# Decode attention with a gated dense layer: GpSimd brings the output projection's chunks with two or four partitions per DMA engine, in whole 32 KB elements

## The chip, the core and the metric

The kernel runs on one core of a Trainium2 chip. The core has TensorE (matrix products), VectorE, ScalarE, GpSimd and SyncE, each with its own instruction queue, and 16 DMA engines that all queues share. The metric is the device time of one execution in microseconds: 192.6 us before, the median of three runs (192.58 to 192.64).

## What is computed

One token is decoded. Branch A is attention of one query against a cache of 4096 positions for 32 heads of 128, followed by the output projection `wo`; branch B is a dense layer with a squared ReLU; a gate mixes the two.

```python
def reference(A_x, A_k_cache, A_v_cache, A_wq, A_wo, B_x, B_w1, B_b1, B_w2, B_b2, gate_w):
    # x [1,1,512], k_cache and v_cache [1,32,4096,128], wq [512,4096], wo [4096,512]
    q = (x @ wq) as [1,32,1,128]
    scores = einsum("bhqd,bhkd->bhqk", q, k_cache) * 128 ** -0.5
    o = einsum("bhqk,bhkd->bhqd", softmax(scores), v_cache)
    a = o as [1,1,4096] @ wo
    h = relu(x @ w1 + b1) ** 2          # w1 [512,1376]
    b = h @ w2 + b2                     # w2 [1376,512]
    g = sigmoid((x * gate_w).sum())
    return g * a + (1 - g) * b          # everything in bfloat16
```

The two caches are 32 MB each; with the weights nearly 79 MB are read, each byte once.

## The kernel before

The heads go in eight tiles of four. For each tile the kernel loads 4 MB of K and 4 MB of V into a ring of five slots (`ring`), 128 partitions of 32 KB each. SyncE issues these loads in the order of `LOADS`, each after the slot's old contents are no longer read (`free`): for a K tile the counts of VectorE and TensorE, for a V tile those of TensorE. Loads are issued well ahead, and the transfers queue.

The scores of a tile are split by position. VectorE does 80 of 128 blocks (96 in the last tile) with a multiply and add along the row (`ttr`, L704); TensorE transposes the rest (L502), ScalarE copies the transposes out of PSUM (L408) and TensorE multiplies them with the query (L515). Then come the maximum (L711, L522, L718, L721, L527), the exponentials on ScalarE (L427) and the products with V on TensorE (`pv`, L546), some two tiles later.

The projection `wo` comes in two parts. Heads 0 to 27 (3.5 MB) are seen as 112 chunks of 32 rows, 32 KB each, and every chunk goes to one partition of `W`, a tile that first holds `wq`. Which chunk lies on which partition is free, since a selection matrix `selA` puts the attention output on the same partitions: `spread_a` multiplies with it (L565), and then TensorE (`out_a`, L573) and VectorE (`rows_v`, L766 and L770) use `W`. The last four heads of `wo` go elsewhere, at the very end, on SyncE's queue (L332), with the last 128 rows of `w2` behind them (L334).

The plan of the chunks is by DMA engine. `INNER` names partitions 32 to 95, engine e having 32 + 4e to 35 + 4e; `OUTER` the partitions 0 to 31 and 96 to 127, also four per engine; `SEAM` is a pair of them (31 and 99). An entry of `RUNS` is a kind, the first engine e, the number of engines k, which of the four partitions r, and in the kernel before a factor m: with m = 2 the run brings two partitions per engine. `place` turns it into first partition, step and count. Engines 0 to 2 are filled by `FIRST`, eight transfers of three chunks each that SyncE issues (L320). Engine 3 gets one chunk, engines 0 to 2, 4, 7 and 8 eight each, and the others seven.

The runs are GpSimd's. A transfer of GpSimd begins at the engine where the one before ended, so `turns` puts in a dummy (L368, a few bytes into `dm`) wherever the next run is to begin elsewhere, with as many engines as are to be skipped. GpSimd first builds `selA` with one `affine_select` per strip (L356), waits until `W` is free and the gate and bias are done (`started`, L310), then issues dummies and runs in order (L368, L371), waits for all of them (L377, L378) and sets `tick` (L379), whose semaphore `s_wk` lets `spread_a` and `rows_v` go on. `max_dma_last_dim=16384` on the runs cuts each 32 KB row into two elements of 16 KB.

SyncE's order around this: wq (L290), three K tiles and the first V tile (L326), the eight transfers of `FIRST` (L320), then the other K and V tiles; V of the last three tiles comes in parts (L324); before the last V come `w1` and `w2` (L329, L330).

Of the kernel before, what the change touches and what calls it, by code (L numbers as in the profile page):

```python
# [5 lines left out]
def bass_gated_mix__gqa_block_cached__dense_activation_squared_relu__decode_kernel(  # L6
# [50 lines left out]
    for i in (28, 29, 30):  # L57
# [20 lines left out]
    TP = 32 - TV  # L78
    TM = 6
    INNER, OUTER, SEAM = range(3)  # L80
    RUNS = [(INNER, 4, 12, 0, 2), (INNER, 4, 12, 1, 2),
            (OUTER, 4, 4, 0, 1), (OUTER, 8, 8, 0, 1), (OUTER, 4, 4, 1, 1), (OUTER, 8, 8, 1, 1),
            (OUTER, 4, 4, 2, 1), (OUTER, 8, 8, 2, 1),
            (OUTER, 3, 2, 3, 1), (SEAM, 7, 2, 3, 1)]
    FIRST = [(INNER, 0, 3, 0, 1), (INNER, 0, 3, 1, 1), (INNER, 0, 3, 2, 1), (INNER, 0, 3, 3, 1),
             (OUTER, 0, 3, 0, 1), (OUTER, 0, 3, 1, 1), (OUTER, 0, 3, 2, 1), (OUTER, 0, 3, 3, 1)]

    def place(kind, e, k, r, m):
        if kind == INNER:
            return 32 + 4 * e + r, 4 // m, k * m  # L90
        if kind == OUTER:
            return (4 * e if e < 8 else 64 + 4 * e) + r, 4, k
        return 28 + r, 68, k

    def turns():
        at, out = 0, []
        for _, e, k, _, _ in RUNS:
            d = (e - at) % 16
            out.append((False, d) if d != 1 else (True, e))
            at = (e + k) % 16  # L100
        return out

    def strips():
        q = 0
        for run in RUNS + FIRST:
            yield (*place(*run), q)
            q += place(*run)[2]
        assert q == 4 * NA

    STRIPS = list(strips())  # L110

    k_v = A_k_cache.rearrange("a (j r) (p b) d -> (a j) (r p) (b d)", r=R, p=P)
    v_v = A_v_cache.rearrange("a (j r) (p b) d -> (a j) (r p) (b d)", r=R, p=P)
    wq_v = A_wq.rearrange("(p t) n -> p (t n)", t=4)
    woa_v = A_wo.rearrange("(p t) n -> p (t n)", t=32)
# [15 lines left out]
    with ctx:  # L131
        def sb(name, shape, dt):
            return ctx.enter_context(nc.sbuf_tensor(name, shape, dt))
# [4 lines left out]
        def sem(name):  # L138
            return ctx.enter_context(nc.semaphore(name))
# [3 lines left out]
        def held(kind, j=0):  # L143
            return ring[:, AT[kind, j] % SLOTS, :]

        W = sb("W", [128, 32 * DM], bf16)
# [32 lines left out]
        o2f = sb("o2f", [128, TV], fp32)  # L179
        dm = sb("dm", [16, len(RUNS), 2, 6], bf16)  # L180
        ident = sb("ident", [128, 128], bf16)
# [54 lines left out]
        s_wo = [sem(f"s_wo{n}") for n in range(len(TS) - 1)]  # L236
        s_wp = [sem(f"s_wp{n}") for n in range(len(RUNS))]
        s_dm = [sem(f"s_dm{n}") for n in range(len(RUNS))]
        s_wr = sem("s_wr")
# [56 lines left out]
        def free(eng, n):  # L296
            if n < SLOTS:
                return
            kind, j = LOADS[n - SLOTS]
            if kind == "k":  # L300
                eng.wait_ge(s_sd, U * (j + 1))
                eng.wait_ge(s_t, 2 * U * (j + 1))
            elif kind == "v":
                eng.wait_ge(s_pv, U * (j + 1))

        def started(eng):
            eng.wait_ge(s_qps, NT)
            eng.wait_ge(s_g, 4)
            eng.wait_ge(s_b1c, 1)  # L310

        @block.sync
        def _(eng):
            for n, (kind, j) in enumerate(LOADS):
                free(eng, n)
                if n == SLOTS - 1:
                    started(eng)
                    for p, st, k, q in STRIPS[len(RUNS):]:
                        eng.dma_start(W[p:p + st * (k - 1) + 1:st, :], woa_v[q:q + k, :]).then_inc(s_wr, 16)  # L320
                if kind == "v" and j in PARTS:
                    for w in range(len(PARTS[j]) - 1):
                        part = slice(PARTS[j][w] * 128, PARTS[j][w + 1] * 128)
                        eng.dma_start(held("v", j)[:, part], v_v[j][:, part]).then_inc(s_vl[j, w], 16)  # L324
                elif kind in "kv":
                    eng.dma_start(held(kind, j), (k_v if kind == "k" else v_v)[j])\  # L326
                       .then_inc(s_l[n % SLOTS], 16)
                elif kind == "m":
                    eng.dma_start(held("m")[:, 0:W2], w1_v).then_inc(s_w[0], 16)  # L329
                    eng.dma_start(held("m")[:, W2:W3], w2_v).then_inc(s_w[1], 16)  # L330
            for c in range(len(TS) - 1):
                eng.dma_start(wob_sb[:, TS[c]:TS[c + 1], :], wob_v[:, TS[c]:TS[c + 1], :])\  # L332
                   .then_inc(s_wo[c], 16)
            eng.dma_start(w2b, B_w2[F - 128:F, :]).then_inc(s_w[2], 16)  # L334
            eng.wait_ge(s_f4, 1)
            eng.dma_start(out[0, 0, :].rearrange("(j p) -> j p", p=128), fin4).then_inc(s_out, 16)

        @block.gpsimd
        def _(eng):  # L340
            eng.memset(ident[:, :], 0.0).then_inc(s_id, 1)
            eng.memset(identf[:, :], 0.0).then_inc(s_id, 1)
            eng.memset(onesf[:, :], 1.0).then_inc(s_cst, 1)
            eng.wait_ge(s_id, 2)
            for m in (ident, identf):
                eng.affine_select(out=m[:, :], in_=m[:, :], compare_op=ALU.not_equal, fill=1.0,
                                  base=0, pattern=[[-1, 128]], channel_multiplier=1)\
                   .then_inc(s_id, 1)
            eng.memset(RS[:, :], 0.0).then_inc(s_cst, 1)
            eng.memset(E[:, :, :, :], 0.0).then_inc(s_cst, 1)  # L350
            eng.memset(selA[:, :, :], 0.0).then_inc(s_sel, 1)
            eng.wait_ge(s_sel, 1)
            for n, (p, st, k, q) in enumerate(STRIPS):
                eng.wait_ge(s_sel, n + 1)
                part = selA[:, :, p:p + st * (k - 1) + 1]
                eng.affine_select(out=part, in_=part, compare_op=ALU.not_equal, fill=1.0, base=-st * q,  # L356
                                  pattern=[[st, 4], [-1, st * (k - 1) + 1]], channel_multiplier=4 * st)\
                   .then_inc(s_sel, 1)

            started(eng)
            sent = 0
            for n, ((back, d), run) in enumerate(zip(turns(), RUNS)):
                if back:
                    eng.inc_swdge_sem([], [], mode="reset_dge_cursor")
                if d:
                    src = B_w1[0:d, 0:32].rearrange("p (a c) -> p a c", a=2)
                    eng.dma_start(dm[0:d, sent, :, 0:4], src[:, :, 0:4]).then_inc(s_dm[sent], 16)  # L368
                    sent += 1
                p, st, k, q = STRIPS[n]  # L370
                eng.dma_start(W[p:p + st * (k - 1) + 1:st, :], woa_v[q:q + k, :],  # L371
                              max_dma_last_dim=16384).then_inc(s_wp[n], 16)
            for n in range(sent):
                eng.wait_ge(s_dm[n], 16)
            eng.wait_ge(s_wr, 16 * len(FIRST))
            for q in s_wp[:-1]:
                eng.wait_ge(q, 16)  # L377
            eng.wait_ge(s_wp[-1], 16)  # L378
            eng.memset(tick[:, :], 0.0).then_inc(s_wk, 1)  # L379
# [461 lines left out]
```

## Time and profile before

| | |
|---|---|
| median of three runs | 192.60 us |
| the profiled execution: its time, its span | 192.64 us, 191.2 us |
| VectorE busy | 158.8 us (83%) |
| TensorE busy | 111.2 us (58%) |
| ScalarE busy | 82.6 us (43%) |
| GpSimd busy | 18.7 us (10%) |
| DMA, mean over the span | 412 GB/s, 78.74 MB in 5300 packets |
| granted TensorE clock | 0.58 |
| GpSimd's DMAs | 17: 10 runs and 7 dummies, issued from 33.8 to 43.8 us |
| `FIRST`, issued by SyncE | 33.5 to 39.2 us |

A line of the waits names who waited, for whom, and how long in all, how often and the longest. A line of the timeline or of the chain starts with the start and the duration in us. The page's queue rows give packets, MB and the share of the time of 16 engines; the trace also keeps each packet's queue, start, duration and size.

### The profile page before, as it was taken

The numbers are of one execution on the slowest core, as the hardware profiler recorded it, in microseconds if no ns is written. First come the engines' busy times: TensorE is split into PE (matmuls) and PEld (weight loads), VectorE is DVE, ScalarE is ACT, GpSimd is POOL, SyncE is SP. The second block draws the span as 40 slices with busy tenths as digits, with TensorE's granted clock in tenths as the row PEclk, the third lists the DMA queues.
The fourth block names the chain that finished last, engine by engine and source line by source line (L and its number), as shares of the span: only waits on it lengthen the run. The fifth ranks groups of instructions, "written<-read, shape, count | busy, mean of one in ns | idle before, by whom it ended". The sixth has DMA issues, their size and how long they took to land.

```text
span 191.2 us, 5991 instructions
## 1 busy us (share of the span) xinstructions
PE 111.2 (58%) x2058; PEld 97.6 (51%) x2058; DVE 158.8 (83%) x1387; ACT 82.6 (43%) x204; POOL 18.7 (10%) x48
## 2 busy tenths in 40 slices
PE   0139567645614653397469254936876478548975
PEld 0123244535503542297359244935866368537964
DVE  0310399999999999999999998999999699998821
ACT  2105675843833663078339232943743393000400
POOL 7630000991000000000000000000000000000000
PEclk9999995855555555555555555555555555555555
DMA  6999999999999999999999999999999999999992
GB/s 220 440 439 439 439 441 429 439 401 454 422 413 418 432 420 418 449 413 446 422 437 422 432 417 411 441 417 439 435 427 429 391 425 413 422 417 425 418 383 82
DMA packets 5300, 78.74 MB, mean 412 GB/s; under 512 B 1099, under 2 KB 1741, under 8 KB 1870
## 3 DMA queue, kind: packets, MB, share of 16 engines
q1 hardware_dynamic: 4488, 75.47, 93.1%
q0 software_dynamic: 768, 2.89, 3.7%
q8 instruction: 16, 0.26, 0.6%
q14 instruction: 14, 0.11, 0.1%
q10 hardware_dynamic: 14, 0.01, 0.0%
HBM read 78.35 MB, written 0.00 MB: 410 GB/s over the span
## 4 chain that ended last, share of the span: by engine, by line
DVE 64%; DMA 25%; SPq 7%; issue 1%; PE 1%; DVEq 0%
DVE ring L704 60%; DMA ring<-in_A_wo_dram 14%; DMA ring<-in_A_k_cache_dram 11%; SPq L324 7%; DVE S L704 3%; DVE gm L718 1%; PE pM L555 1%; DVE gx L721 0%; PE pQ L607 0%; DVE mp L711 0%; SPq L330 0%; DVE rden L728 0%; SPq L290 0%; SPq L329 0%; DVE qcol L693 0%
## 5 line engine op out<-in xcount | busy, mean ns | idle before, releaser
L704 DVE CUSTOM_DVE_ANT_0 ring<-ring,qb 128x128 bf16<-128x128 bf16 x656 | 140.6, 283 | 1.8 <-DMA ring<-in_A_k_cache_dram 1.8
L408 ACT ACTIVATE kT<-KP 128x768 bf16<-128x768 bf16 (+1 forms) x64 | 46.4, 783 | 47.2 <-PE KP L502 46.9
L502 PE MATMUL KP<-ident,ring 128*128 128x128 bf16 x368 | 43.5, 302 | 18.9 <-DMA ring<-in_A_k_cache_dram 15.7
L704 DVE DVE_READ_ACCUMULATOR2_ANT S<- 128x1 f32 x656 | 52.0, 79 | 0.1
L502 PEld LDWEIGHTS KP<-ident,ring 128*128 128x128 bf16 x368 | 36.0, 140 | 21.5 <-DMA ring<-in_A_k_cache_dram 16.1
L546 PE MATMUL pO<-E,ring 128*128 128x4 bf16 x640 | 19.5, 166 | 3.8 <-DMA ring<-in_A_v_cache_dram 2.1
L546 PEld LDWEIGHTS pO<-E,ring 128*128 128x128 bf16 x640 | 18.7, 105 | 4.3 <-DMA ring<-in_A_v_cache_dram 2.4
L427 ACT ACTIVATE E<-S,nM 32x128 bf16<-32x128 f32 x32 | 18.5, 579 | 1.0
L546 PE MATMUL pX<-E,ring 128*128 128x4 bf16 x384 | 12.0, 167 | 4.7 <-DMA ring<-in_A_v_cache_dram 4.7
L546 PEld LDWEIGHTS pX<-E,ring 128*128 128x128 bf16 x384 | 11.4, 105 | 5.2 <-DMA ring<-in_A_v_cache_dram 5.1
L522 PE MATMUL pM<-identf,mp 128*1 128x128 f32 x8 | 3.0, 379 | 14.5 <-DVE mp L711 14.5
L419 ACT ACTIVATE nM<-pM 128x1 f32<-128x1 f32 x8 | 1.4, 171 | 23.0 <-PE pM L527 23.0
L527 PE MATMUL pM<-onesf,gx 1*128 1x1 f32 x16 | 4.7, 358 | 9.0 <-DVE gx L721 9.0
L527 PEld LDWEIGHTS pM<-onesf,gx 1*128 1x128 f32 x16 | 4.0, 307 | 9.6 <-DVE gx L721 9.6
L522 PEld LDWEIGHTS pM<-identf,mp 128*1 128x1 f32 x8 | 0.7, 85 | 16.0 <-DVE mp L711 15.8
L515 PE MATMUL pQ<-qcol,kT 128*128 128x4 bf16 x176 | 7.8, 170 | 1.0 <-ACT kT L408 0.9
L515 PEld LDWEIGHTS pQ<-qcol,kT 128*128 128x128 bf16 x176 | 7.6, 111 | 1.3 <-ACT kT L408 1.3
L515 PE MATMUL pS<-qcol,kT 128*128 128x4 bf16 x192 | 8.1, 169 | 0.0
L427 ACT ACTIVATION_READ_ACCUMULATOR E<-S,nM 32x1 f32 x32 | 8.1, 253 | 0.0
L515 PEld LDWEIGHTS pS<-qcol,kT 128*128 128x128 bf16 x192 | 7.9, 108 | 0.2
L399 ACT ACTIVATE qb<-pQ 32x128 bf16<-32x128 f32 x16 | 4.3, 268 | 7.8 <-PE pQ L480 7.5
L555 PE MATMUL pM<-RS,onesf 128*128 128x8 f32 (+1 forms) x10 | 2.9, 358 | 7.8 <-DVE gm L718 6.6
(83 smaller groups left out, 94.2 us busy)
## 6 DMA issues: line engine op xcount, KB each, us to landing
ring<-in_A_k_cache_dram SPq DMA_DIRECT2D x8, 4096.0 KB, 29.9
ring<-in_A_v_cache_dram SPq DMA_DIRECT2D x5, 4096.0 KB, 29.0
W<-in_A_wq_dram SPq DMA_DIRECT2D x1, 4096.0 KB, 12.2
ring<-in_A_v_cache_dram SPq DMA_DIRECT2D x2, 2048.0 KB, 27.5
ring<-in_A_v_cache_dram SPq DMA_DIRECT2D x4, 1024.0 KB, 28.2
ring<-in_A_v_cache_dram SPq DMA_DIRECT2D x2, 1280.0 KB, 32.3
W<-in_A_wo_dram POOLq DMA_DIRECT2D x2, 768.0 KB, 18.1
ring<-in_B_w_dram SPq DMA_DIRECT2D x1, 1376.0 KB, 25.7
```

Source lines behind the costliest of these rows:

```text
L324: eng.dma_start(held("v", j)[:, part], v_v[j][:, part]).then_inc(s_vl[j, w], 16)
L399: eng.activation(qb[rows, c, :], QR[c % 2][rows, r * 128:r * 128 + 128], ACT.Copy)\
L408: eng.activation(kT[:, n % NC, 0:HB[u // U] * 128], KP[n % 3][:, 0:HB[u // U] * 128], ACT.Copy).then_inc(s_ev, 1)
L427: eng.activation(E[rows, j % NE, :, r], S[rows, j % NS, :], ACT.Exp, bias=nM[rows, j:j + 1], scale=SCALE, accum_out=RS[rows, R * j + r:R * ...
L502: mm = eng.transpose(KP[n % 3][:, y * 128:(y + 1) * 128], held("k", j)[:, b * 128:(b + 1) * 128], ident[:, :])
L515: mm = eng.matmul(S2[j % 2][:, c:c + R], kT[:, n % NC, y * 128:(y + 1) * 128], qcol[:, R * j:R * j + R], start=True, stop=True)
L522: eng.transpose(MT[0:1, :], mp[:, j:j + 1], identf[:, :]).then_inc(s_mt, 1)
L527: eng.matmul(MB[:, j:j + 1], gx[0:1, j % 2, :], onesf[0:1, 0:1], start=True, stop=True).then_inc(s_mb, 1)
L546: mm = eng.matmul(O(R * j, R * j + R), held("v", j)[:, b * 128:(b + 1) * 128], E[:, j % NE, b, :], start=(b == 0), stop=(b == B - 1), skip ...
L555: eng.matmul(DEN[:, a:b], onesf[:, :], RS[:, a:b], start=True, stop=True).then_inc(s_den, 1)
L704: ins = eng.tensor_tensor_reduce(kb, kb, qb[:, j, :], 1.0, 0.0, ALU.mult, ALU.add, S[:, j % NS, b:b + 1])
L718: eng.tensor_reduce(g, MT[0:1, :].rearrange("a (r p) -> a r p", r=R), AX.X, ALU.max)\
```

## The change

`RUNS` names the partitions of an engine as a tuple: the first run brings all four `INNER` partitions of engines 4 to 15 (48 chunks in one transfer), the next two bring partitions 0 and 2 of the `OUTER` group, and four runs of one partition per engine remain. Seven runs are left, and `turns` then gives five dummies. For a run of several partitions the source rows are rearranged so that its outermost dimension counts the engines and the next one the partitions of each; the destination is one strip of partitions. The rows are no longer cut: `max_dma_last_dim` is gone, and an element is 32 KB. Which partition belongs to which engine, and how many chunks each engine gets, is as before; which chunk lies on which partition changes, and `selA` is built from `ROWS`, which has a strip for each partition index r of a run: 12 strips for the runs and 8 for `FIRST`, where there were 10 and 8.

```diff
-    RUNS = [(INNER, 4, 12, 0, 2), (INNER, 4, 12, 1, 2),
-            (OUTER, 4, 4, 0, 1), (OUTER, 8, 8, 0, 1), (OUTER, 4, 4, 1, 1), (OUTER, 8, 8, 1, 1),
-            (OUTER, 4, 4, 2, 1), (OUTER, 8, 8, 2, 1),
-            (OUTER, 3, 2, 3, 1), (SEAM, 7, 2, 3, 1)]
+    RUNS = [(INNER, 4, 12, (0, 1, 2, 3)), (OUTER, 4, 4, (0, 2)), (OUTER, 8, 8, (0, 2)),
+            (OUTER, 4, 4, (1,)), (OUTER, 8, 8, (1,)), (OUTER, 3, 2, (3,)), (SEAM, 7, 2, (3,))]
...
+    def place(kind, e, k, rs):
+        r, m = rs[0], len(rs)
+        if kind == SEAM:
+            return 28 + r, 68, k, m
+        p = 32 + 4 * e + r if kind == INNER else (4 * e if e < 8 else 64 + 4 * e) + r
+        return p, 4 // m, k, m
...
     STRIPS = list(strips())
+    ROWS = [(p + st * r, st * m, k, q + r * k) for p, st, k, m, q in STRIPS for r in range(m)]
...
-            for n, (p, st, k, q) in enumerate(STRIPS):
+            for n, (p, st, k, q) in enumerate(ROWS):
                 eng.wait_ge(s_sel, n + 1)
...
-                p, st, k, q = STRIPS[n]
-                eng.dma_start(W[p:p + st * (k - 1) + 1:st, :], woa_v[q:q + k, :],
-                              max_dma_last_dim=16384).then_inc(s_wp[n], 16)
+                p, st, k, m, q = STRIPS[n]
+                rows = woa_v[q:q + k * m, :]
+                if m > 1:
+                    rows = rows.rearrange("(r i) n -> i r n", r=m)
+                eng.dma_start(W[p:p + st * (k * m - 1) + 1:st, :], rows).then_inc(s_wp[n], 16)
```

## The prediction

> **What bounds the kernel now.** I read the DMA row of the slices and the queue rows first, then the chain of waits, the table of waits, GpSimd's timeline, the busy time by stage, and last the single DMA packet records of the trace.
>
> ```profile
> DMA  6999999999999999999999999999999999999992
> ...
> DMA packets 5300, 78.74 MB, mean 412 GB/s; under 512 B 1099, under 2 KB 1741, under 8 KB 1870
> ...
> q1 hardware_dynamic: 4488, 75.47, 93.1%
> q0 software_dynamic: 768, 2.89, 3.7%
> ```
>
> The 16 DMA engines are at 90% or more in every slice but the first and the last. q1 is SP's queue (the caches, the weights); q0 is GpSimd's, with 3.7% of the engines' time. The busy time by stage says it closer:
>
> ```profile
> 80.00:100.00 20.00, 13.62 (x255) 13.11 (x255) 19.33 (x177) 10.74 (x23) 0.00 (x0) 0.50 1.00 425
> 100.00:148.00 48.00, 31.00 (x696) 30.08 (x696) 47.33 (x439) 24.08 (x55) 0.09 (x1) 0.50 1.00 428
> 148.00:188.40 40.40, 28.63 (x668) 26.20 (x665) 31.48 (x227) 10.70 (x34) 0.00 (x0) 0.50 0.97 401
> ```
>
> The last two columns are DMA share and GB/s. The share is 1.00 up to 148 us, and 0.97 in the last stretch, in which some engines finish early. VectorE (third pair, 47.33 of 48 us) is nearly full as well, so which of the two decides has to be settled at the end:
>
> ```profile
> 153.32 8.75 SPq L324
> 162.11 26.10 DMA ring<-in_A_wo_dram
> 188.34 0.56 PE pQ L607 x16
> 188.90 0.28 PE pQ L598 x4
> ```
>
> From 162.11 us the chain is one DMA that waits its turn behind the queue, then half a microsecond of TensorE on each last weight. The issues say the same: SP issues w1 (L329) at 148.54 us and it lands at 174.21, that is 25.7 us later for 1.4 MB. So some 22 us of work lie in the queues when VectorE frees that slot; VectorE could be that much later before an engine ran dry. **The end is the end of the DMA engine with the most work.** What an edit does to the time is what it does to that engine's sum.
>
> The records carry no engine number, but on one engine a packet starts 3 to 4 ns before the end of the one before, so 16 chains can be followed, and each engine's order of sizes on q1 is known from the code. The chain with a single wo chunk is engine 3 (it has one in the plan). It ends last, at 188.42 us. It is the one that carries nine 8 KB instruction fetches, each of 0.31 us and followed by a 32 KB packet of 1.87 instead of 1.21 us. Five more chains end at 188.32, 188.20, 188.13, 188.06 and 188.03; the earliest three at 184.9 to 185.9. So six engines end within 0.4 us of each other, and no gain on one of them alone reaches 0.4 us.
>
> **What q0 consists of.** Its 768 records are 176 of 16 KB, 480 of 4 B, 87 of 8 B and 25 of 16 B. That is: each run puts two 16 KB records per chunk on the engines with data (88 chunks, 176 records), one 4 B record on each of the engines without, and a 4 B count on all 16; each dummy puts three small records on all 16. With 64 places where a run has data on an engine, 10 runs and 7 dummies give 160 + (160 - 64) + 7 x 48 = 592 small ones: the count of the trace. In the chains, q0 and q1 take turns record by record: one of q0, then one 32 KB packet of q1.
>
> **The change, part by part.**
>
> Ten runs and seven dummies become seven and five. The same 88 chunks go to the same engines; by the same sum there are 7 x 16 + (112 - 40) + 5 x 48 = 424 small records and 88 of 32 KB, so 512 in place of 768: 16 fewer per engine in the mean. For engine 3 (one chunk, in the run of two) it is 42 to 29: 12 small ones and one cut of a chunk.
>
> What a record costs: 9 ns by its own length for a small one, 5.5 ns if the 3.5 ns of overlap are taken off. A chunk as 2 x 611 ns against 1213 ns (the median of SP's 32 KB packets) is 9 ns less, or 5.5 ns with the overlap. Along one chain, six K/V packets with eight small records between them took 7.34 us where six alone take 7.26, that is 10 ns each, with the scatter of the large ones in it. So engine 3 saves 13 x 5.5 = 0.07 to 13 x 10 = 0.13 us; I take 0.10. An engine with seven chunks (50 to 33 records) saves 0.09 to 0.17; I take 0.14, so engine 3 stays last. **Sum: 0.10 us less, at the end of the span.**
>
> [...]
>
> GpSimd's issue: five DMAs less on its queue.
>
> ```profile
> 33.81 0.74 POOL L368 DMA_DIRECT2D dm<-in_B_w_dram  x1 [21.92 <-PE pX L480]
> 34.55 0.62 POOL L371 DMA_DIRECT2D W<-in_A_wo_dram  x1
> ...
> 43.22 0.55 POOL L371 DMA_DIRECT2D W<-in_A_wo_dram  x1
> 100.36 0.09 POOL L379 MEMSET tick<- 1x1 f32 x1 [56.59 <-DMA W<-in_A_wo_dram]
> ```
>
> At 0.55 to 0.62 us each that is 2.9 us of GpSimd, which then waits 56.6 us for the data anyway: nothing. The table of selections becomes 20 operations in place of 18: two 47-wide ones (0.38 and 0.36 us, 0.5 us from one to the next) become four 45-wide ones, so 1.0 us more of GpSimd ahead of its wait of 21.92 us: nothing; without that cover it would be 1.0 us later DMAs, still ahead of need. The tick itself comes earlier: q0's records take turns with q1's, so with 17 fewer turns of 1.22 us it comes near 81 us instead of 100.4. Its readers, TensorE's spread and VectorE's sums, come at 173: nothing.
>
> What moves: the 8.5 us of wo per engine are spent by about 80 us, not spread to 99. SP's packets in between come later. The load to look at is K of tile 3, which lands at 72.13 us; about 21 turns of q0 precede it. By then an engine has moved up to 6 chunks before the change and up to 7 after, so it lands one packet, 1.2 us, later: 73.4. VectorE begins tile 3 at 75.61, so 2.2 us remain. TensorE starts its transposes at 72.18, on that landing; it goes 1.2 us later, ends near 89.5 instead of 88.2, and then waits until 91.5 for K of tile 4 as now. That K lands at 91.47 with nearly all chunks moved in both kernels. So nothing of it reaches the end, and VectorE's own waits stay:
>
> ```profile
> POOL tick L379 <- DMA W<-in_A_wo_dram: 56.6, 1, 56.6
> ...
> DVE ring L704 <- DMA ring<-in_A_k_cache_dram: 1.8, 2, 1.6
> ```
>
> If the cover were gone, a late K would cost VectorE its lateness, but the time only if it exceeded the 22 us of queued work.
>
> The profiled execution took 192.64 us, with a span of 191.17 and 1.47 around it; the median is 192.60. So 192.64 - 0.10 = 192.54 for that one, **192.5** against the median.
>
> **Rivals.**
>
> 1. *The runs do not land on the planned engines* (slower). The 48-partition run is written as 12 groups of 4 on the source side and as 48 partitions on the other. Were it spread over 16 engines with three partitions each, engine 3, already last, would get three chunks more: 3 x 1.21 = 3.6 us, and the time would be 196.2. It decides from the first whole chunk more on one of the six late engines (1.2 us, less its 0.1 to 0.4 of slack: 193.4). For it: 16 divides 48, and the old runs of 24 fit 12 engines by either way of counting. Against it: in the old runs 12 engines do carry exactly two, beginning at engine 4, and three chains carry no q0 data at all; the slowest dimension of the source is 12, as written out. [...] Chance 0.08.
>
> 2. *A large record of q0 holds q1 up more than two halves do* (slower), by K landing late or by longer packets. SP's 32 KB packets average 1222.9 ns between 60 and 100 us beside q0 and 1224.2 between 100 and 150 almost without it, so sharing costs nothing; the lateness is priced above. One more collision like those behind the fetches (0.65 us) on a late engine would give 193.1. Chance 0.07.
>
> 3. *Small records cost more than their length* (faster). For 0.4 us at the end every one of the six late engines would have to save that, 0.4/17 = 24 ns per record, over twice the most that a chain shows; or the fetches would fall otherwise. Time 192.1. Chance 0.13.
>
> 4. *The elements are still cut at 16 KB*, so that only dummies and runs go: 12 small records on engine 3, 0.07 to 0.12 us: 192.5 as well. Chance 0.04, within the no-change case.
>
> **Numbers.** The forecast has 0.68 and rival 4 0.04, so no change (within 0.2%, 0.39 us, about what a measurement of this kernel can tell) has 0.72; faster 0.13; slower 0.15. The likeliest case alone gives 192.4 to 192.6. For 8 in 10, the range reaches to rival 3's 192.1 and rival 2's 193.1: 192.0 to 193.1; the rest, mostly rival 1, is left out.
>
> **What would show it.** q0's row: 512 packets, 2.89 MB, 3.6%; q1 unchanged. Twelve DMAs on GpSimd's timeline, the last issued near 40 us, the tick near 81. K of tile 3 landing near 73.4, VectorE's first wait for K no longer than now. DMA share still 1.00 up to 148 us and the last landing 0.1 us before 188.85. I am wrong if a chain gains or loses a chunk, if q0 and q1 no longer take turns record by record, or if a late engine loses whole packets' time.

## The result and the profile after

The changed kernel takes 202.69 us (median of five runs, 202.54 to 203.21) against 192.64 us for the kernel before on the same chip (192.58 to 192.77): a ratio of 1.052, with a 95% interval of 1.0508 to 1.0531. That is 10.05 us slower. The forecast was 192.5, and its range ended at 193.1.

The page of the changed kernel, the DMA rows (engines' busy tenths and GB/s in 40 slices of 5.03 us, then packets, MB and time by queue):

```profile
DMA  6999999999999999999999999999999999999940
GB/s 235 444 463 423 417 412 440 430 448 427 384 262 313 313 305 430 443 430 428 433 423 412 420 438 436 433 443 417 417 428 410 417 415 419 421 416 422 399 165 19
...
q1 hardware_dynamic: 4488, 75.47, 90.8%
q0 software_dynamic: 464, 2.89, 4.3%
```

The engines are as busy as before, but from the 11th slice to the 15th they move 262 to 384 GB/s where the other slices move about 425. They work all the time and get less done. q1's packets are the same 4488. q0 has 464 packets, not the 512 forecast, and takes more of the engines' time (4.3%) although it has fewer packets and the same bytes. The last slice but one moves 165 GB/s: some engines have finished and others have not.

Busy time by stage, after (stretch, its length, pairs of busy time and count for PE, PEld, DVE, ACT, POOL, then clock, DMA share, GB/s):

```profile
40.00:53.00 13.00, 7.66 (x99) 7.06 (x99) 12.84 (x119) 7.81 (x20) 0.00 (x0) 0.50 1.02 434
53.00:66.00 13.00, 4.96 (x60) 4.48 (x58) 12.86 (x120) 4.96 (x12) 0.00 (x0) 0.50 1.01 311
66.00:76.00 10.00, 2.65 (x65) 2.29 (x62) 9.97 (x94) 4.22 (x10) 0.00 (x0) 0.50 1.00 311
76.00:100.00 24.00, 11.49 (x229) 11.20 (x229) 16.84 (x155) 9.22 (x21) 0.09 (x1) 0.50 1.00 428
```

The same two stretches in the kernel before:

```profile
53.00:66.00 13.00, 4.97 (x60) 4.46 (x57) 12.86 (x118) 4.96 (x12) 0.00 (x0) 0.50 1.03 437
66.00:76.00 10.00, 4.02 (x76) 3.49 (x74) 9.90 (x95) 5.65 (x12) 0.00 (x0) 0.50 0.99 420
```

The rate is lost between 53 and 76 us, at a DMA share of 1.00. The first 13 us of the table above, in which the 48-chunk run goes out, are undisturbed at 434 GB/s. VectorE loses its time only behind it: 16.84 of 24 us.

The waits and the end of the chain, after:

```profile
POOL tick L382 <- DMA W<-in_A_wo_dram: 44.9, 1, 44.9
...
DVE ring L707 <- DMA ring<-in_A_k_cache_dram: 12.0, 6, 6.6
```

```profile
163.59 8.66 SPq L325
172.30 25.94 DMA ring<-in_A_wo_dram
198.37 0.57 PE pQ L610 x16
198.95 0.28 PE pQ L601 x4
```

VectorE waits 12.0 us for K, where it was 1.8. The tail is the old one, 10 us later. GpSimd's queue did what was forecast: twelve DMAs, the last at 39.48 us, and the tick at 84.85.

**In the packet records.** Up to 53 us a 32 KB packet takes 1.21 us, as before. Between 53.5 and 76 us, packets of all 16 engines take up to 2.4 us: 144 packets of 32 KB are over 1.5 us between 36 and 110 us, against 10 before. Summed over the engines, the 32 KB records between 36 and 110 us take 109.3 us more than at 1213 ns each (before: 10.4, with q0's 16 KB records counted against 611 ns), that is 6.8 us per engine against 0.65. I call this sum the excess below.

The chains of records also show where the chunks went. Two of the chains that carry `FIRST` have four chunks of q0 each, at 53.9, 57.6, 62.7 and 67.3 us in one of them, where the plan has none. The chains of engines 8 to 15 have six chunks in place of seven or eight, those of engines 4 to 7 seven. The four runs of one partition per engine had gone elsewhere: one partition per engine from engine 0 on. 4 + 8 + 2 + 2 chunks dealt that way give engines 0 and 1 four each, 2 and 3 two each, 4 to 7 one each, which is what the chains hold. The three data records of the fourth dummy lie on chains of engines 4 to 6, so the cursor had not moved either. And the 48 packets that are missing from the forecast 512 are the ones that these four runs would have put on engines without data (12 + 8 + 14 + 14).

**Which engine ends last.** From the last 16 KB packet of V on, every engine has the same packets of q1 left, about 27.9 us of them. That packet ends at 170.57 and 169.44 us on the two chains with `FIRST` and four chunks of q0, at 167.27 on the third chain with `FIRST`, and at 166.14 on engine 3's, which is known by its 8 KB instruction fetches. These chains end at 198.48, 197.35, 195.19 and 196.01 us; engine 3's takes 29.9 us for the rest, with two more fetches in it. So it is one of engines 0 and 1 that ends the kernel now, and no longer engine 3.

In the trace's own notation, a run of one partition per engine now has the shape [4,1], [8,1] or [2,1] of 32 KB elements; before, it was [2,4], [2,8] or [2,2] of 16 KB. The grouped runs have [1,48], [1,8] and [1,16], with a source of two dimensions in the code, and they landed on plan.

### The profile page after: what moved, and what is told of

Read it like the earlier page. It is cut to its first block, busy times and chain, and to the rows that moved or that the text cites. A ratio compares the mean times of both kernels' runs of the same rounds, so it can differ in the third digit from the quotient of the medians.

```text
span 201.2 us, 5987 instructions
## 1 busy us (share of the span) xinstructions
PE 108.8 (54%) x2058; PEld 96.2 (48%) x2058; DVE 159.3 (79%) x1387; ACT 82.6 (41%) x204; POOL 16.2 (8%) x45
## 4 chain that ended last, share of the span: by engine, by line
DMA 61%; DVE 29%; SPq 6%; PE 2%; issue 1%
DMA ring<-in_A_k_cache_dram 48%; DVE ring L707 26%; DMA ring<-in_A_wo_dram 13%; SPq L325 6%; DVE S L707 1%; PE pO L549 1%; PE KP L505 0%; DVE gx L724 0%; DVE gm L721 0%; PE pQ L610 0%; SPq L331 0%; SPq L291 0%; PE pM L530 0%; SPq L330 0%; PE KP L663 0%
## 5 line engine op out<-in xcount | busy, mean ns | idle before, releaser
L505 PE MATMUL KP<-ident,ring 128*128 128x128 bf16 x368 | 42.4, 295 | 38.7 <-DMA ring<-in_A_k_cache_dram 35.3
L505 PEld LDWEIGHTS KP<-ident,ring 128*128 128x128 bf16 x368 | 34.8, 137 | 41.4 <-DMA ring<-in_A_k_cache_dram 35.7
L707 DVE DVE_READ_ACCUMULATOR2_ANT S<- 128x1 f32 x656 | 51.0, 78 | 0.1
L773 DVE SCALAR_TENSOR_TENSOR ring<-W,o2f,ring 128x512 f32<-128x512 bf16 x9 | 6.8, 751 | 0.3
L696 DVE CAST qcol<-pM 128x4 bf16<-128x4 f32 x8 | 1.3, 159 | 6.5 <-PE pM L490 6.5
```

What stands on the lines that cost most here:

```text
L505: mm = eng.transpose(KP[n % 3][:, y * 128:(y + 1) * 128], held("k", j)[:, b * 128:(b + 1) * 128], ident[:, :])
L707: ins = eng.tensor_tensor_reduce(kb, kb, qb[:, j, :], 1.0, 0.0, ALU.mult, ALU.add, S[:, j % NS, b:b + 1])
L773: eng.scalar_tensor_tensor(out=vsum[:, :], in0=wo_sb[:, TP + t, :], scalar=o2f[:, t:t + 1], in1=vsum[:, :], op0=ALU.mult, op1=ALU.add).the ...
```

## The experiments

The theory after the result had two parts. A: a run of single partitions in whole rows is dealt from engine 0 on. P: a chunk that one engine writes into partitions that the plan gives to another engine slows the queue.

**1. Cut the single runs again.**

```diff
+                cut = {} if m > 1 else {"max_dma_last_dim": 16384}
-                eng.dma_start(W[p:p + st * (k * m - 1) + 1:st, :], rows).then_inc(s_wp[n], 16)
+                eng.dma_start(W[p:p + st * (k * m - 1) + 1:st, :], rows, **cut).then_inc(s_wp[n], 16)
```

> The changed kernel, with the rows of the runs of one partition per engine cut at 16 KB again; the runs of two and four stay whole. Theory A (a run of single partitions in whole 32 KB elements is dealt one partition per engine from engine 0 on, whatever the cursor says, and does not move the cursor): the plan holds again, engines 0 and 1 lose their four extra chunks, no K or V packet over 1.9 us but those behind instruction fetches, time 192.3 to 192.8. Rival B (the grouped runs or their whole elements slow the queue): stays at 201 to 204.

Measured: 192.54 us against 192.74, ratio 0.9993 (0.9984 to 1.0002). The 10 us are gone; the grouped runs of whole rows stayed. Its stages (same columns):

```profile
53.00:66.00 13.00, 4.97 (x59) 4.45 (x57) 12.86 (x118) 4.97 (x12) 0.00 (x0) 0.50 1.02 434
66.00:76.00 10.00, 4.00 (x76) 3.48 (x74) 9.90 (x95) 5.63 (x12) 0.00 (x0) 0.50 1.00 422
```

434 and 422 GB/s where the changed kernel had 311 and 311. The excess is 10.0 us, the old one. Rival B falls: neither the grouping nor the whole elements of the grouped runs cost anything that the interval shows.

**2. Take the cut off the single runs of the kernel before**, and nothing else.

```diff
+                cut = {"max_dma_last_dim": 16384} if run[4] > 1 else {}
                 eng.dma_start(W[p:p + st * (k - 1) + 1:st, :], woa_v[q:q + k, :],
-                              max_dma_last_dim=16384).then_inc(s_wp[n], 16)
+                              **cut).then_inc(s_wp[n], 16)
```

> The kernel before, with only the cut at 16 KB taken off its eight runs of one partition per engine (28 and more chunks keep their runs of two, cut). Theory A: these runs are dealt from engine 0 on; engines 0 and 1 hold 16 chunks each in place of 8, and 28 of the 40 or so chunks of single runs are written into other engines' partitions, so worse than the changed kernel: 205 to 214 us. Rival B (the grouping by the rearranged source is what costs): 192.3 to 192.9 us.

Measured: 213.58 us against 192.64, ratio 1.1085 (1.1068 to 1.1103), with an excess of 219.2 us. So this one argument does the damage by itself, without any of the rest of the change, and more with 40 chunks in such runs than with 16. Dealt from engine 0 on as in the changed kernel, all 40 are written into other engines' partitions, and engines 0 and 1 carry 16 chunks each in place of eight; q0's 640 packets fit that dealing (96 and 40 with data, 168 small ones of the runs and 336 of the dummies).

**3. Planned counts, other engines' partitions.** As experiment 1, but the two single runs of `OUTER` change places, with the cursor kept, so that every engine from 4 to 15 still brings one chunk.

```diff
-            (OUTER, 4, 4, (1,)), (OUTER, 8, 8, (1,)), (OUTER, 3, 2, (3,)), (SEAM, 7, 2, (3,))]
+            (OUTER, 8, 8, (1,)), (OUTER, 4, 4, (1,)), (OUTER, 3, 2, (3,)), (SEAM, 7, 2, (3,))]
...
-        for _, e, k, _ in RUNS:
+        for (_, e, k, _), e in zip(RUNS, (4, 4, 8, 4, 12, 3, 7)):
```

> As e1, every engine with the same number of chunks as in the plan, but the two single runs change places: engines 4 to 11 write the partitions of engines 8 to 15, and engines 12 to 15 those of engines 4 to 7 (12 chunks). Theory P (a chunk written into partitions that another engine's K and V packets are being written to slows all engines): packets near 2 us around these chunks and 194 to 198 us. Rival I (only the number of chunks per engine counts): as e1, 192.3 to 192.8.

Measured: 196.39 us against 192.74, ratio 1.0179 (1.0153 to 1.0206); excess 53.2 us. The profiled execution, 195.28 us, is the fastest of the four. Its stages:

```profile
53.00:66.00 13.00, 4.97 (x60) 4.46 (x58) 12.86 (x120) 4.97 (x12) 0.00 (x0) 0.50 1.01 399
66.00:76.00 10.00, 4.01 (x76) 3.48 (x74) 9.94 (x94) 4.68 (x11) 0.00 (x0) 0.50 1.01 351
```

No engine has a chunk too many, and it is 3.7 us slower: P holds, and rival I, that only the count of chunks matters, falls.

**4 and 5. The whole runs, with and without crossing.** Both leave out `FIRST` and its wait (24 chunks of the projection are not brought). One is otherwise the changed kernel; in the other the four single runs go to partitions of the engines on which they are dealt.

```diff
-    FIRST = [(kind, 0, 3, (r,)) for kind in (INNER, OUTER) for r in range(4)]
+    FIRST = []
...
-            (OUTER, 4, 4, (1,)), (OUTER, 8, 8, (1,)), (OUTER, 3, 2, (3,)), (SEAM, 7, 2, (3,))]
+            (OUTER, 0, 4, (0,)), (OUTER, 0, 8, (1,)), (OUTER, 0, 2, (2,)), (OUTER, 0, 2, (3,))]
```

(The second pair of lines is experiment 5 alone; its dummies stay those of the changed kernel.)

> The changed kernel without the eight transfers of FIRST (24 chunks are left out, its output is not the whole projection), so engines 0 and 1 hold four chunks and not twelve. Theory P: the slow stretch near 53 to 76 us stays, 197 to 200 us. Rival I: engine 3, with two chunks, is last again, 193 to 194 us.

> As e4 (24 chunks left out), but the four single runs go to the partitions of engines 0 to 7 on which they are dealt (whole elements still, the same engines, the same count). Theory P: no slow stretch, 192.5 to 194 us. Rival R (single runs in whole elements are slow by themselves, wherever they go): as e4.

Measured: 201.24 us (1.0453, 1.0418 to 1.0487) without `FIRST`, 194.13 us (1.0072, 1.0058 to 1.0086) on own partitions. Experiment 4 was above its range: taking 24 chunks off engines 0 to 2 brought only 1.5 us. Engine 3 is the last engine in both (its chain ends at 196.07 and at 189.55 us). The stages from 53 to 76 us, first of experiment 4:

```profile
53.00:66.00 13.00, 4.96 (x58) 4.45 (x57) 12.86 (x120) 4.96 (x12) 0.00 (x0) 0.50 0.99 323
66.00:76.00 10.00, 2.56 (x65) 2.42 (x65) 9.90 (x93) 4.01 (x10) 0.00 (x0) 0.50 1.02 356
```

and of experiment 5:

```profile
53.00:66.00 13.00, 4.97 (x61) 4.54 (x58) 12.86 (x120) 4.95 (x12) 0.00 (x0) 0.50 1.01 432
66.00:76.00 10.00, 4.18 (x77) 3.51 (x75) 10.00 (x96) 5.80 (x12) 0.00 (x0) 0.50 1.00 422
```

The same transfers, whole rows, the same engines, the same number; only the partitions differ, and the slow stretch is there or not (excess 98.7 and 9.6 us). Rival R, that single runs in whole elements are slow wherever they go, falls. The pair puts the price of crossing at 201.24 - 194.13 = 7.1 us, for engine 3. What remains in experiment 5 is 194.13 - 192.74 = 1.4 us: engine 3 has two chunks there in place of one, one packet of 1.21 us.

**6. Two chunks only.** As experiment 1, without the last dummy, so that engines 5 and 6 bring the two chunks of `SEAM` into partitions of engines 7 and 8. Engines 5 and 6 then have one chunk more than planned, and 7 and 8 one less.

```diff
             at = (e + k) % 16
+        out[-1] = (False, 0)
         return out
```

> As e1, without the last dummy: the last run's two chunks are brought by engines 5 and 6 into partitions of engines 7 and 8, and the others stay as planned. Theory C (while one engine writes into another's partitions, all 16 slow down): some 10 us or more of packet time above 1.21 us summed over the engines near these two chunks, 192.9 to 193.8 us. Rival S (only the two engines that share a port slow, by a packet each): 5 us or less in sum, 192.3 to 192.7 us.

Measured: 194.39 us against 192.64, ratio 1.0087 (1.0073 to 1.0101), above both ranges. Its stages around the two chunks:

```profile
70.00:76.00 6.00, 1.46 (x12) 1.20 (x12) 6.00 (x58) 2.20 (x6) 0.00 (x0) 0.50 1.01 427
76.00:80.30 4.30, 1.21 (x33) 1.06 (x33) 4.20 (x38) 0.00 (x0) 0.00 (x0) 0.50 1.04 343
```

For 4.3 us the rate falls from 427 to 343 GB/s. In the records, some 40 packets of 32 KB that start in this stretch take 1.3 to 1.8 us, two or three on each engine, those that share no partitions with anyone among them. The excess is 26.3 us, 16.3 more than in experiment 1; with sharing between two engines alone it would be about two packets of 1.21 us per chunk, 4.8, an estimate. Theory C (all 16 engines slow down) holds, and rival S (only the two that share) falls. Why the time grows by 1.75 us when the excess per engine grows by 1.0 was not found.

**7 and 8. Does it matter which partitions?** As experiment 1, with the run of eight split in two runs of four. In the first, engines 8 to 11 and 12 to 15 swap their partitions; in the second, engines 4 to 7 and 8 to 11. Eight chunks cross in each.

```diff
-            (OUTER, 4, 4, (1,)), (OUTER, 8, 8, (1,)), (OUTER, 3, 2, (3,)), (SEAM, 7, 2, (3,))]
+            (OUTER, 4, 4, (1,)), (OUTER, 12, 4, (1,)), (OUTER, 8, 4, (1,)), (OUTER, 3, 2, (3,)), (SEAM, 7, 2, (3,))]
...
-        for _, e, k, _ in RUNS:
+        for (_, e, k, _), e in zip(RUNS, (4, 4, 8, 4, 8, 12, 3, 7)):
```

(These are the lines of experiment 7; in experiment 8 the three runs begin at 8, 4 and 12.)

> As e1, with the run of eight single partitions split in two runs of four that change places: engines 8 to 11 write the partitions of engines 12 to 15 and the other way round. Eight chunks cross, all within partitions 96 to 127, with every engine's count as planned. If any crossing slows all engines (theory C): 194 to 197 us and a stretch of packets near 1.7 us. If only crossing between the lower and the upper 64 partitions does it (theory H): 192.3 to 193.0 us.

> As e9, but engines 4 to 7 write the partitions of engines 8 to 11 and engines 8 to 11 those of engines 4 to 7: again eight chunks cross, now all between the lower and the upper 64 partitions. Theories C and H both: 194 to 197 us.

Measured: 195.31 us (1.0138, 1.0112 to 1.0164) and 195.41 us (1.0150, 1.0128 to 1.0173), excess 57.5 and 53.6 us. It makes no difference whether the chunks stay within the upper partitions: theory H, that only crossing between the lower and the upper 64 costs, falls.

**9. A dimension of one.** The rearranged source for single runs too, rows whole.

```diff
-                if m > 1:
-                    rows = rows.rearrange("(r i) n -> i r n", r=m)
+                rows = rows.rearrange("(r i) n -> i r n", r=m)
```

> The changed kernel with the same rearranged source for the single runs too (a dimension of one is put in, rows whole). If the written shape decides how a run is dealt, and it survives, the plan holds: 192.3 to 192.9 us. If a run of single whole rows is dealt from engine 0 however it is written: 201 to 204 us.

Measured: 202.81 us, ratio 1.0525 (1.0503 to 1.0547). In the trace the shapes are [4,1], [8,1] and [2,1] as in the changed kernel: the dimension did not survive, so this tells nothing of a shape that would.

No version beats the kernel before by more than its interval; experiment 1 equals it.

## Why the prediction was wrong

**What bounds the kernel** held in kind: the end is the end of the engine with the most work. But "engine 3 stays last" did not. The chain that ends at 198.48 us, one of engines 0 and 1, has `FIRST`'s eight chunks and four of q0. In the kernel before it ended near 187.6 us (its last 16 KB packet at 159.61), 0.9 us ahead of engine 3's 188.42. It is now 10.9 us later: four chunks at 1.21 us make 4.9, and its 32 KB records between 36 and 110 us exceed 1213 ns by 6.9 us in sum, where it was 0.6. Less the 0.9 us that it had to spare, this is the loss, 198.48 - 188.42 = 10.06 us.

**The step that failed** is the one that says "The same 88 chunks go to the same engines". The prediction's own sign of being wrong, a chain that gains or loses a chunk, is what happened. I read the sentence off `place` and `turns`, which both assume that a run starts at the cursor and divides by the written dimension. For 72 of the 88 chunks that holds. For the 16 in single runs, dropping the cut changed more than the size of an element: it took away the second dimension of the transfer, and with it the way the transfer is dealt. Experiments 1 and 2 show that the cut decides; what in the shape does it was not separated, since experiment 9 left the shape as it was. Costing the cut as 5.5 to 10 ns per chunk priced the element and not the shape.

**Rival 1** had the right family of mechanism, runs that do not land on the planned engines, but pinned it to the wrong run. I looked at the run that was new (48 partitions) and not at the four that seemed to lose only an argument; the run of 48 landed on plan. Its price, whole chunks on one engine, was nearly half of what happened: four chunks, 4.9 us, on an engine with 0.9 us to spare, where the rival had three on engine 3 for 3.6 us. Without crossing, one chunk more on engine 3 cost 1.4 us (experiment 5).

**The other term** was in no rival: writing into other engines' partitions, 6.3 us on the last chain, 7.1 us on engine 3 in experiments 4 and 5. "Sharing costs nothing", from the K and V packets beside q0, was true of what the trace of before could show, in which every chunk went to its own engine's partitions, and experiment 1 confirms it there. (By the time of the span, the two means in the prediction are 1222.4 and 1225.0 ns; its windows lay 10.7 us earlier.) It does not carry over to crossing. For engine 3 the two terms make 7.1 + 1.4 = 8.5 of the 10.05 us. The other 1.5 appears when `FIRST` is there too (202.69 against 201.24): engine 3's chain ends at 196.01 us with it and at 196.07 without, but with `FIRST` another engine ends 2.4 us behind it. No run has the misplaced chunks with `FIRST` and without crossing, so the two terms of the last engine are read from its chain alone.

**What held.** The sum for the intended change, 0.10 us less, fits experiment 1, which is what I had costed but for the cut of 16 chunks: 0.9993 (0.9984 to 1.0002) contains it, and zero as well, so no run tells it from nothing. GpSimd's issue time, the two more selections and the earlier tick cost nothing; the tick came at 84.85 us, against 81 forecast (17 turns of 1.22 us from 100.4 give 79.6; 81 fits 16), and at 82.8 in experiment 1. The cover that I gave for a late K held too: K of tile 3 landed 10.8 us later (82.89 us) and VectorE waited 6.6 us for it, but the DMA share stayed at 1.00, so that wait is a mark of the loss and not its cause.

## What to carry to other kernels

When engines are assigned by hand, dropping a size argument can change the shape of the transfer and with it the engines that carry it, as it did here: check the number of packets on the queue and the chunks per chain before believing the plan. When a DMA-bound stretch slows down at a DMA share of 1.00, as here from some 430 to 311 GB/s, look at the length of single packets, and compare them on engines that have nothing to do with the change. Ask again which engine ends last after a change; it need not be the one from before. Keep a side transfer on the engine to which the plan gives its partitions; a balanced load did not make up for crossing (196.39 us in experiment 3, 192.54 in experiment 1).

## What the runs showed of the hardware that was not expected

The transfers of GpSimd's with one whole 32 KB element per partition and plain lists of 2, 4 or 8 partitions on both sides went to engines 0, 1, 2 and so on (four, four, two, two and then one chunk each on the chains), left the cursor where it was (the fourth dummy lies on engines 4 to 6), and put no filler on the other engines (464 packets where 512 were counted on). With two elements per partition they started at the cursor: in the kernel before, the chains hold the plan's chunks of q0 (none on three, one on one, eight on three, seven on nine), and experiment 1 has 528 packets, the 512 and one more for each of the 16 cut chunks.

A 32 KB chunk written by one engine into another's partitions by the plan, while K and V went to all of them, slowed all 16: in the changed kernel the packets under way at 55.5 us took over 1.5 us on each of the 16, where 1.21 is the median up to 53. The excess per crossing chunk was 3.6 us (12 chunks at once, experiment 3), 5.5 and 5.9 (eight, experiments 8 and 7), 6.2 (16, the changed kernel), 5.2 (40, experiment 2) and 8.1 (two, experiment 6), each after taking off about 10 us that are there without crossing; sharing by two engines alone would make 2.4, by the estimate of experiment 6. Why engines with partitions of their own slow down stays open; nothing here looked at the path itself.

The plan gives an engine four neighbouring partitions and the four 32 higher. In experiments 3 to 5 it counted whether the chunks kept to this plan: 196.39 us with 12 chunks off it, 201.24 with 16 off it and 194.13 with 16 in the same transfers on it. No other map was tried.
